# A chunked recurrence followed by a routed MoE: TensorE's steps reordered, scores of b in full quarters, old states by transposes

## The chip, the cores and the metric

The kernel runs on one core of one Trainium2 chip, in fp32. The metric is the device time of one execution in microseconds. The kernel before takes 818.32 us, the median of three runs (818.29, 818.32 and 825.19). The engines have short names in the profile: PE is TensorE, DVE is VectorE, ACT is ScalarE, POOL is GpSimd and SP is SyncE, which only issues transfers; PEld are TensorE's weight loads.

## The reference

There are two parts, one after the other. The first is a recurrence over S = 768 steps, for each of B = 4 batches and H = 8 heads, with a state of D x D = 40 x 40:

```
y[t]  = r[t] . state
Sa    = state . a[t]
state = state * w[t] - outer(Sa, b[t]) + outer(v[t], k[t])
```

Its output y, seen as B*S = 3072 tokens of H*D = 320 features, is the input of a mixture of experts. There are 8 experts, and a token's expert is fixed by a hash of its id, `token_ids * 2654435761 % 8`. Each expert computes `relu(x @ w1[e]) @ w2[e]` with an inner size of 1024.

## The kernel before

**Chunks.** The recurrence isn't walked step by step. The sequence is cut into 12 chunks of C = 64 tokens, and the batches into two pairs, which makes 24 tiles, u = 2n + g for chunk n and pair g; a tile has 16 heads (2 batches of 8). Within a chunk, cumulative products of the decays w (called p and q, q being taken from the other end) are multiplied onto a, b and k. Then the chunk's inner recurrence is a triangular system: the scores of b against a make a 64x64 unit triangular matrix per head, which is inverted and applied to a right side, built from the old state (r0) and from the chunk's own v and the scores of k (r1). The result c gives the new state (s) and, with the scores of r (rc_v for v, rc_c for c), the output y.

**The inverse.** A 64x64 triangle is treated as two diagonal blocks of BLK = 32 and one block below them. The diagonal blocks of four tiles (a group) are inverted together on VectorE, by 31 links of two instructions each (group_i, lines 506 and 509), with 128 partitions that hold 2 batches x 2 blocks x 32 rows. The transposes ut and ug of the result (lines 517, 518) feed the block below the diagonal, in two TensorE steps called x and u.

**The pipeline.** Tile u has an early part A (tile_a): its loads, the products with p and q, its transposes (at_t of a, z of b and k), and the scores a, from which ScalarE copies pk (the scores of b), GpSimd copies no (the part of pk below the diagonal blocks) and VectorE makes mk (the masked scores of k). Its late part runs LAG = 8 ticks later: tile_s (r and v, transposed in the step rv), tile_m (x and u) and tile_b (r0, r1, c, nc, rc, s, y, sd). nc are c's transposes, which go to the right operand of s; sd are the transposes of the decayed state sc, for the y of a later tick. So in ticks 8 to 23 every tick has part A of one tile and part B of another, and in the last eight ticks only part B.

**The order of the work.** Each piece is registered at a time, counted in ticks, by `at_tick`. The plan is sorted by that time and emitted in this order, and each engine executes its instructions in the order of emission. Within a tick the list STEPS (line 128) orders TensorE's steps; a step's copies by ScalarE, and what VectorE and GpSimd do for it, are emitted with it. The order of other work (loads, decays, the group's links) is set by numbers such as `t0 - 2`, `u - 2.3`. A TensorE step that has to wait holds all steps that follow.

**Decays.** p and q are made in rounds of two chunks (decays, lines 249 to 357), six in all. A round loads w, clamps it, makes prefix products on pb and suffix products on qb within segments (the chain; on VectorE for rounds 0 and 1, on GpSimd for later ones), takes the segments' products (own), combines them over TensorE (ends), and multiplies these into the segments (spread). Round 0 is turned on chip; later rounds are stored to p_rows and q_rows in memory by SP's queue, and each tile loads its part back (pl and ql). The code's instruction packets arrive by a queue of their own.

**PSUM.** The pool psa has two slots of two banks (for t_ps, z_ps, a_ps, c_ps and rc_ps), psb two slots of one bank (all other results of TensorE), psu one for the inverse. A slot is free for a new result when the copy that reads it is done.

**MoE.** From about 537 us the kernel loads the experts' weights, gathers each expert's tokens with indirect transfers and runs the two matmuls of each expert.

Of the kernel before, what the change touches and what calls it, by code (L numbers as in the profile page):

```python
# [8 lines left out]
F32 = mybir.dt.float32  # L9
I32 = mybir.dt.int32  # L10
AF = mybir.ActivationFunctionType
OP = mybir.AluOpType
# [6 lines left out]
def kernel(  # L19
# [108 lines left out]
    STEPS = ["c", "rc_v", "sd", "nc", "rc_c", "u", "a", "rv", "s", "x", "y", "z", "r0", "at_t", "r1"]  # L128
# [23 lines left out]
    for lo, hi, when in ((0, 4, -9.0), (4, LAG, -3.0), (LAG, NZ, 3.0)):  # L152
        @at_tick(when)
        def _(lo=lo, hi=hi):
            nc.gpsimd.memset(z_all[:, lo:hi].rearrange("p i b hp (two x) -> p (i b hp two) x", two=2)[:, :, D:C], 0.0)
# [4 lines left out]
    rv_r = ring("rv", 1, [P, 2, 3, HP, C])  # L160
    at_t_r = ring("at_t", LAG, [P, 2 * HP * C + BLK], lambda t: t[:, 2 * HP * C:], 4)
    r1_r = ring("r1", 2, [P, HP, R], gaps)
    r_r = ring("r", 2, [P, HP, P], gaps, 2)
# [4 lines left out]
    @at_tick(3.0)  # L168
    def _():
        nc.gpsimd.memset(x_all[:].rearrange("p i b hp (two x) -> p (i b hp two) x", two=2)[:, :, D:C], 0.0)  # L170
# [78 lines left out]
    def decays(ri, t_load, t0, t_own, t1):  # L249
# [3 lines left out]
        chain = nc.gpsimd if ri > 1 else nc.vector  # L253
# [10 lines left out]
        def clamp():  # L264
            chain.tensor_scalar(x["qb"][:, 0:HC * D], x["pb"][:], LO, HI, op0=OP.max, op1=OP.min)
            (nc.vector if fast else nc.gpsimd).memset(segs(x["pb"])[:, :, 0, :], 1.0)
# [39 lines left out]
        def turned(i, src):  # L306
# [4 lines left out]
            if i == 0:  # L311
                nc.scalar.copy(hi[half(0)], lo[half(1)])
                nc.scalar.copy(lo[half(1)], lo[half(0)])
            else:
# [6 lines left out]
        def finish():  # L321
            eng = nc.vector if fast else nc.gpsimd
            if fast:
                spread(eng, x["qb"][:], x["ends"][:, 1:])
                turned(0, x["qb"][:, D:])
                recip()
                spread(eng, x["pb"][:], x["own"][:])
                turned(1, x["pb"][:])
                return
            recip()  # L330
            for i, (t, by, src) in enumerate((("pb", x["own"][:], x["pb"][:]), ("qb", x["ends"][:, 1:], x["qb"][:, D:]))):
                spread(eng, x[t], by)
                for y in range(2 * RN):
                    nc.sync.dma_start(pq_dram[ri][i][y * HC:(y + 1) * HC].rearrange("t bh e -> bh t e"),
                                      src[y * BH:(y + 1) * BH].rearrange("p (t e) -> p t e", e=D))

        first_half = [clamp] + [lambda i=i: prefix(i) for i in range(1, SL)]
        second = [lambda i=i: suffix(i) for i in range(SL - 2, -1, -1)]
        if ri > 1:
            first_half += second  # L340
            second = []
        for i, f in enumerate(first_half):
            at_tick(t0 + (t_own - t0) * i / len(first_half), order=8)(f)
        at_tick(t_own, order=8)(own)
        for i, f in enumerate(second):
            at_tick(t_own + (t1 - t_own) * (i + 0.5) / (len(second) + 1), order=8)(f)
        at_tick(t1 - 0.05, order=8)(ends)
        at_tick(t1, order=8)(finish)

        @at_tick(t1 + 0.6, order=8)  # L350
# [12 lines left out]
    def tile_a(u):  # L363
# [8 lines left out]
        if early:  # L372
            t_in, t_pq, t_mul = -8.9 + 0.01 * u, None, -6.0 + 0.01 * u
            t_turn, t_a = u - 1, u + 0.9 if u < 3 else u + 0.4
        elif second:
            base = 4 + 0.7 * (u - 4)
            t_in, t_pq, t_mul, t_turn, t_a = u - 2.3, 3.4 + 0.01 * u, base - 0.5, base - 1, base + 0.4
        else:
            t_in, t_pq, t_mul, t_turn, t_a = u - 2.3, u - 2.7, u - 1.7, u - 1, u + STEPS.index("a") / len(STEPS)

        @at_tick(t_in)
        def _():
            x["z"] = z_r(u)
            x["at"] = r_r(1) if u == 3 else at_r(u)
# [22 lines left out]
        @at_tick(t_mul)  # L407
        def _():
            eng = nc.vector if early else nc.gpsimd
            if early:  # L410
                p, q = (rounds[0][i][rn] for i in "pq")
                x["p"] = p[:, (2 * g + rn) * DM:(2 * g + rn + 1) * DM]
# [3 lines left out]
            times(eng, x["at"][:], x["p"])  # L416

        @at_tick(t_turn, "at_t")
        def _():
            t = at_t_r(u)  # L420
            x["at_f"] = t
            x["at_t"] = t[:, 0:2 * HP * C].rearrange("p (b hp t) -> p b hp t", b=2, hp=HP)
# [3 lines left out]
            nc.scalar.copy(t[0:R, 0:2 * HP * C].rearrange("p (b c) -> p b c", b=2), p[0:R, :, 0:HP * C])  # L426

        @at_tick(t_turn, "z")
        def _():
            if early and u % 2:  # L430
                x["z_t"] = rv_r(0)[:, :, 0:2]
            else:
                x["z_t"] = work.tile([P, 2, 2, HP, C], F32, tag="z_t", name="z_t", bufs=1)
            p = psum("z_ps")
            for i in range(2):
                for be in range(2):
                    for hp in range(HP):
                        c0 = (be * HP + hp) * C
                        nc.tensor.transpose(p[0:R, i, c0:c0 + C], x["z"][half(i), be, hp, 0:R], ident[half(i), half(i)])  # L439
            nc.scalar.copy(x["z_t"][0:R].rearrange("p i b hp t -> p i (b hp t)"), p[0:R])  # L440

        @at_tick(t_a)
        def _():
            gi, ti = divmod(u, GRP)
            p = psum("a_ps")
            for hp, par, be in quarters():
                z = x["z_t"][half(par), be, be, hp, :]
                c0 = (be * HP + hp) * C
                for i in range(2):
                    r0 = be * C + i * BLK  # L450
                    mm(p[r0:r0 + BLK, par, hp * C:(hp + 1) * C], z[:, i * BLK:(i + 1) * BLK],
                       x["at_f"][half(par), c0 + i * BLK:c0 + i * BLK + C])
            for hp, par, be in quarters():
# [624 lines left out]
```

## Time and profile before

The profiled execution took 824.48 us, with a span of 822.7 us and a mean granted TensorE clock of 0.888.

| | us | share of the span |
|---|---|---|
| span | 822.7 | |
| PE busy | 653.1 | 79% |
| DVE busy | 324.1 | 39% |
| POOL busy | 282.4 | 34% |
| ACT busy | 259.1 | 31% |
| start, to the first y at 142.8 | 142.8 | 17% |
| 15 ticks with both parts, 142.8 to 437.2 | 294.4 | 36% |
| 8 ticks with part B alone, to 534.8 | 97.6 | 12% |
| MoE, to the end | 287.9 | 35% |

The rows of the stages were read from TensorE's timeline, by the start of each tile's y. Busy time is time in which an engine executes; the share of an engine over the whole span is a mean over these four stages. The granted clock is the share of its full speed at which TensorE was allowed to run. Its value in a short stretch is close to 0.5 or to 1.0. A line of a timeline gives the start, the duration, the engine, the source line, the operation, its output and inputs with their partitions x elements, the count of instructions, and in brackets the idle time before it and what ended that. Durations of neighbouring TensorE steps overlap a little, so that a step's cost is better taken from its start to the start of the next.

### The profile page before, as it was taken

To read this page: it belongs to the slowest core of one execution; us is meant where nothing else is said; L and a number is where in the kernel's file an instruction comes from. 1 tells how busy PE (TensorE), PEld (TensorE's weight loads), DVE (VectorE), ACT (ScalarE), POOL (GpSimd) and SP (SyncE) were. 2 spreads that over 40 slices of the span, in tenths; PEclk is the share of its full clock that TensorE was granted. 3 is DMA by queue.
4 is the path that set the end of the run, shared out by engine and by line. 5 is a ranking of instruction groups with operands and counts; after the bars stand their busy time and mean duration, and the time that the engine had idled before them with its cause. 6 is when DMAs were issued, how large, how long until landed. Compare 5 with 4: busy or idle time off the path is not lost.

```text
span 822.7 us, 27069 instructions
## 1 busy us (share of the span) xinstructions
PE 653.1 (79%) x11982; PEld 498.9 (61%) x11982; DVE 324.1 (39%) x709; ACT 259.1 (31%) x518; POOL 282.4 (34%) x372
## 2 busy tenths in 40 slices
PE   0534366979798898788888989929999999999993
PEld 0423355868687877677776878815555655655652
DVE  6674644663664356346525742211441101111110
ACT  0622233445444454455534445501011011111110
POOL 3057785264437464334212212240302202210101
PEclk9999997787878679899858879968989999999997
DMA  9455776634664477444212223188841343220000
GB/s 159 100 90 126 129 138 105 150 82 84 121 149 86 74 115 142 94 85 89 39 33 41 42 55 65 39 290 265 283 136 39 112 148 102 95 88 16 24 3 27
DMA packets 201896, 83.47 MB, mean 101 GB/s; under 512 B 177518, under 2 KB 192367, under 8 KB 201776
## 3 DMA queue, kind: packets, MB, share of 16 engines
q1 hardware_dynamic: 189008, 64.32, 36.3%
q0 software_dynamic: 6336, 16.08, 6.6%
q10 hardware_dynamic: 6432, 1.31, 1.0%
q8 instruction: 95, 1.56, 0.8%
q14 instruction: 25, 0.20, 0.1%
HBM read 66.56 MB, written 15.44 MB: 100 GB/s over the span
## 4 chain that ended last, share of the span: by engine, by line
PE 65%; DVE 9%; issue 9%; SPq 4%; POOL 4%; ACT 4%; DMA 3%; POOLq 0%; ACTq 0%; DVEq 0%
PE dn_ps L913 11%; PE up_ps L893 9%; PE r_ps L220 6%; PE y_ps L220 5%; PE s_ps L220 5%; PE rc_ps L220 4%; PE a_ps L220 4%; PE u_ps L220 3%; PE t_ps L475 3%; PE up_ps L889 3%; PE z_ps L439 3%; PE c_ps L220 3%; PE sd_ps L220 2%; PE nc_ps L635 2%; POOL xg L872 1%
## 5 line engine op out<-in xcount | busy, mean ns | idle before, releaser
L913 PE MATMUL dn_ps<-w,ht 128*128 128x320 f32 x384 | 104.9, 433 | 0.0
L893 PE MATMUL up_ps<-xt,w 128*128 128x416 f32 x256 | 96.0, 529 | 0.0
L913 PEld LDWEIGHTS dn_ps<-w,ht 128*128 128x128 f32 x384 | 72.8, 190 | 32.1 <-issue 1.9
L903 POOL DMA_INDIRECT out_dram<-o,idx_all x26 | 25.8, 992 | 189.6 <-ACT o L902 184.8
L684 POOL DMA_DIRECT2D x_rows<-xs x48 | 26.8, 562 | 157.2 <-DVE xs L681 105.0
L893 PEld LDWEIGHTS up_ps<-xt,w 128*128 128x128 f32 x256 | 48.5, 195 | 47.6 <-issue 47.6
L509 DVE TENSOR_TENSOR ub<-ub,outer 128x31 f32<-128x31 f32 (+15 forms) x186 | 65.0, 349 | 6.4
L439 PE MATMUL z_ps<-ident,z_all 64*128 64x64 f32 x384 | 34.8, 289 | 40.8 <-POOL z_all L405 31.0
L646 DVE TENSOR_TENSOR mr<-rc_ps,after 128x1024 f32<-128x1024 f32 x24 | 29.4, 1225 | 92.4 <-PE rc_ps L220 92.4
L506 DVE TENSOR_TENSOR outer<-ub,nb 128x31 f32<-128x31 f32 (+15 forms) x186 | 62.8, 338 | 4.2 <-ACT ub L491 0.3
L896 DVE TENSOR_SCALAR ht<-up_ps 128x416 f32<-128x416 f32 x32 | 18.9, 591 | 96.1 <-PE up_ps L893 91.7
L439 PEld LDWEIGHTS z_ps<-ident,z_all 64*128 64x128 f32 x384 | 29.8, 189 | 44.4 <-POOL z_all L405 33.3
L220 PE MATMUL a_ps<-at_t,z_t 64*32 64x64 f32 (+1 forms) x2112 | 40.1, 251 | 15.8 <-issue 9.4
L878 DVE COPY xt<-xg_ps 128x384 f32<-128x384 f32 x24 | 12.1, 551 | 101.7 <-PE xg_ps L877 94.2
L220 PEld LDWEIGHTS a_ps<-at_t,z_t 64*32 64x32 f32 (+1 forms) x2112 | 32.9, 132 | 21.9 <-issue 12.2
L440 ACT COPY z_t<-z_ps 128x1024 f32<-128x1024 f32 x22 | 22.3, 1012 | 70.7 <-PE z_ps L439 70.7
L405 POOL TENSOR_TENSOR z_all<-z_all,ql 128x320 f32<-128x320 f32 x40 | 34.1, 864 | 28.1 <-DMA z_all<-in_k_dram 22.2
L902 ACT COPY o<-dn_ps 128x320 f32<-128x320 f32 x24 | 10.2, 426 | 101.6 <-PE dn_ps L913 101.6
L872 POOL DMA_INDIRECT xg<-x_rows,src_all x26 | 27.3, 1050 | 29.8 <-PE xg_ps L877 15.7
L898 ACT ACTIVATE ht<-up_ps 128x416 f32<-128x416 f32 x32 | 15.9, 515 | 65.3 <-PE up_ps L893 65.3
L889 PE MATMUL up_ps<-xt,w 64*128 64x416 f32 x128 | 30.6, 580 | 7.1 <-DVE xt L878 3.2
L220 PEld LDWEIGHTS s_ps<-x_all,z_all 128*64 128x64 f32 x704 | 27.7, 159 | 13.6 <-issue 13.6
(190 smaller groups left out, 1228.8 us busy)
## 6 DMA issues: line engine op xcount, KB each, us to landing
w<-in_moe_w_dram SPq DMA_DIRECT2D x8, 1280.0 KB
w<-in_moe_w_dram SPq DMA_DIRECT2D x8, 1024.0 KB
ql<-q_rows SPq DMA_DIRECT2D x40, 160.0 KB
r<-in_r_dram SPq DMA_DIRECT2D x48, 80.0 KB
x_all<-in_v_dram SPq DMA_DIRECT2D x48, 80.0 KB
py<-p_rows POOLq DMA_DIRECT2D x48, 80.0 KB
x_rows<-xs POOLq DMA_DIRECT2D x48, 80.0 KB
wt<-in_w_dram SPq DMA_DIRECT2D x6, 640.0 KB
```

What stands on the lines that cost most here:

```text
L220: nc.tensor.matmul(out_, lhsT=lhsT, rhs=rhs, start=start, stop=stop, skip_group_check=True)
L405: eng.tensor_tensor(t, t, by.rearrange("p (h e) -> p h e", e=D), op=OP.mult)
L439: nc.tensor.transpose(p[0:R, i, c0:c0 + C], x["z"][half(i), be, hp, 0:R], ident[half(i), half(i)])
L506: nc.vector.tensor_tensor(tv, ub[:, 0:j + 1, j:j + 1].to_broadcast([P, j + 1, m]), nb[:, j, j + 1:].unsqueeze(1).to_broadcast([P, j + 1, m ...
L509: nc.vector.tensor_tensor(o, o, tv, op=OP.add)
L646: nc.vector.tensor_tensor(t[:].rearrange("p two h t -> p (two h) t"), p[:].rearrange("p two (h t) -> p (two h) t", t=C), after[:].unsqueez ...
L684: nc.gpsimd.dma_start(x_rows[r0:r0 + C, :], xs[half(be)])
L872: nc.gpsimd.indirect_dma_start(out=xg[:, 0:DM], out_offset=None, in_=x_rows[:], in_offset=bass.IndirectOffsetOnAxis(ap=idx, axis=0))
L889: nc.tensor.matmul(banks[-1][:], lhsT=w1[rows, w:w + P], rhs=xt[rows, 2, 0:n], start=True, stop=False)
L893: nc.tensor.matmul(p[:], lhsT=w1[:, c * F + f * P:c * F + (f + 1) * P], rhs=xt[:, c, 0:n], start=False, stop=(c == 1))
L903: st = nc.gpsimd.indirect_dma_start(out=out[:], out_offset=bass.IndirectOffsetOnAxis(ap=idx, axis=0), in_=o[:], in_offset=None, bounds_che ...
L913: nc.tensor.matmul(p[:], lhsT=ht[:, f, j * P:(j + 1) * P], rhs=w2[:, f, :], start=(f == 0), stop=(f == FP - 1))
```

## The change

**The order of the steps.** STEPS goes from `c, rc_v, sd, nc, rc_c, u, a, rv, s, x, y, z, r0, at_t, r1` to `c, z, rcc, nc, rcv, s, a, y, x, sd, r0, at_t, u, r1, rv`. The step x runs one tick before its tile's part B instead of two, and u late in the same tick. z of a tile is in the same tick as its a, and at_t in the tick before. rcc precedes rcv, and the mask product mr follows the latter.

**Scores of b.** In the profile a matmul of fp32 is two instructions and a transpose one. The step a had 32 matmuls for the scores of b, each making 32 of a quarter's 64 rows, and 16 of 64x64 for those of k (96 instructions); now both kinds are 16 full 64x64 matmuls (64 instructions). So the lower diagonal blocks lie in other columns than before, and ScalarE brings them to their place: it copies pk's 32 columns and then, for each batch, the lower rows again from shifted columns. The part no, which GpSimd copied from pk, is now copied by ScalarE from PSUM.

**Old states.** sd was 16 small matmuls (32 instructions) with the identity as the right operand, in a slot of psb; it is now 8 transposes, in a slot of psa.

**r, v and c.** The tile rv is split: the transposes of r go to rt, those of v into a tile cv that c is also copied to. ScalarE makes two copies of half the size where it had one. The transposes of c (nc) read cv.

**Decays and the start.** The parts of a round get times of their own (t_clamp, t_chain, t_own, t_ends, t_spread, t_store). The clamp of rounds 2 to 5 moves from GpSimd to VectorE. Round 2's own, ends, spread and store come after the elimination of group 0, which itself is planned over ticks 3.43 to 6.4. Stores of later rounds come about 0.8 of a tick later. The first tiles' loads, transposes and products, and two fills with zero on GpSimd, are planned in another order.

```diff
-    STEPS = ["c", "rc_v", "sd", "nc", "rc_c", "u", "a", "rv", "s", "x", "y", "z", "r0", "at_t", "r1"]
+    STEPS = ["c", "z", "rcc", "nc", "rcv", "s", "a", "y", "x", "sd", "r0", "at_t", "u", "r1", "rv"]
...
-    def decays(ri, t_load, t0, t_own, t1):
+    def decays(ri, t_load, t_clamp, t_chain, t_own, t_ends, t_spread, t_store):
...
-            chain.tensor_scalar(x["qb"][:, 0:HC * D], x["pb"][:], LO, HI, op0=OP.max, op1=OP.min)
+            nc.vector.tensor_scalar(x["qb"][:, 0:HC * D], x["pb"][:], LO, HI, op0=OP.max, op1=OP.min)
...
-            t_in, t_pq, t_mul, t_turn, t_a = u - 2.3, 3.4 + 0.01 * u, base - 0.5, base - 1, base + 0.4
+            t_in, t_pq, t_mul = (0.55, 0.97, 0.2, 1.05)[u - 4], 3.1 + 0.05 * (u - 4), base - 0.5
+            t_mulz = t_mul
+            t_z, t_at, t_a = base - 0.3, base - 0.15, base + 0.4
         else:
-            t_in, t_pq, t_mul, t_turn, t_a = u - 2.3, u - 2.7, u - 1.7, u - 1, u + STEPS.index("a") / len(STEPS)
+            t_in, t_pq, t_mul = u - 2.3, max(u - 2.4, 6.9 + 0.02 * (u - 8)), max(u - 1.7, 7.0)
+            t_mulz = t_mul
+            t_z, t_at, t_a = (u - i + STEPS.index(n) / len(STEPS) for i, n in ((0, "z"), (1, "at_t"), (0, "a")))
...
-            for hp, par, be in quarters():
-                z = x["z_t"][half(par), be, be, hp, :]
-                c0 = (be * HP + hp) * C
-                for i in range(2):
-                    r0 = be * C + i * BLK
-                    mm(p[r0:r0 + BLK, par, hp * C:(hp + 1) * C], z[:, i * BLK:(i + 1) * BLK],
-                       x["at_f"][half(par), c0 + i * BLK:c0 + i * BLK + C])
-            for hp, par, be in quarters():
-                mm(p[half(1 - be), par, (HP + hp) * C:(HP + hp + 1) * C], x["z_t"][half(par), 1 - be, be, hp, :],
-                   x["at_t"][half(par), be, hp, :])
+            for kind in range(2):
+                for hp, par, be in quarters():
+                    i = be ^ kind
+                    c0 = (kind * HP + hp) * C
+                    mm(p[half(i), par, c0:c0 + C], x["z_t"][half(par), be, hp, i, :], x["at_t"][half(par), be, hp, :])
...
-            nc.scalar.copy(pk.rearrange("p two hp t -> p two (hp t)"), p[:, :, 0:HP * C])
...
-            nc.gpsimd.tensor_copy(no[:], pk[:, :, :, BLK:C])
+            nc.scalar.copy(pk, pb[..., 0:BLK])
+            for be in range(2):
+                low = slice(be * C + BLK, (be + 1) * C)
+                nc.scalar.copy(pk[low], pb[low, :, :, BLK:])
...
+            nc.scalar.copy(no[:], pb[..., BLK:])
...
-        @at_tick(t0 - 2, "x")
+        @at_tick(t0 - 1, "x")
...
-            nc.scalar.copy(t[0:R, :, odd:odd + 2].rearrange("p i j hp t -> p i (j hp t)"), p[0:R])
+            nc.scalar.copy(t[:].rearrange("p b hp t -> p b (hp t)"), p[:, :, 0:HP * C])
+            nc.scalar.copy(cv[:, :, 2:4].rearrange("p hp b t -> p b hp t"),
+                           p[:, :, HP * C:].rearrange("p b (hp t) -> p b hp t", hp=HP))
...
-                p = bank([P, 2 * HP * D], "sd_ps")
+                p = psum("sd_ps")
...
-                        for par in range(2):
-                            rows = half(par)
-                            mm(p[half40(par), (be * HP + hp) * D:(be * HP + hp + 1) * D], sc[rows, be, hp, :],
-                               ident[rows, half40(par)])
+                        nc.tensor.transpose(p[0:D, be, hp * R:(hp + 1) * R], sc[:, be, hp, :], ident[:])
...
-    decays(0, -9.0, -8.0, -7.5, -7.0)
-    decays(1, -8.5, 0.1, 1.9, 3.35)
-    decays(2, 0.0, 3.36, 4.85, 5.2)
+    decays(0, -9.0, -8.0, (-7.9, -7.6), -7.7, -7.4, -7.2, None)
+    decays(1, -8.5, 0.1, (0.15, 1.85), 1.88, 2.2, 2.65, 2.7)
+    decays(2, -5.5, 0.45, (0.5, 2.5), 6.41, 6.43, 6.5, 6.6)
     for ri in range(3, NR):
-        decays(ri, ri * RN * NG - 7.0, ri * RN * NG - 6.3, ri * RN * NG - 4.2, ri * RN * NG - 4.0)
+        t = ri * RN * NG
+        decays(ri, t - 5.8, t - 5.3, (t - 5.2, t - 3.9), t - 3.75, t - 3.6, t - 3.55, t - 3.2)
...
-        group_i(gi, t0 + 0.05, t0 + 0.1, t0 + (3.0 if gi == 0 else 3.15))
+        if gi == 0:
+            group_i(gi, 3.43, 3.47, 6.4)
+        else:
+            group_i(gi, t0 + 0.05, t0 + 0.1, t0 + 3.1)
```

## The prediction

> **What bounds the kernel now.** I read the busy shares of the span first (PE 79%, DVE 39%, POOL 34%, ACT 31%), then the stages, which differ. Columns of the stretches: window, busy us of PE, PEld, DVE, ACT and POOL, granted clock, DMA share.
> ```profile
> core 0: us, PE busy (x) PEld busy (x) DVE busy (x) ACT busy (x) POOL busy (x), PEclk, DMA share, GB/s
> 0.00:142.80 142.80, 62.57 (x1494) 52.60 (x1494) 81.17 (x182) 44.40 (x86) 78.82 (x109) 0.96 0.65 121
> 142.80:437.20 294.40, 252.38 (x6948) 221.69 (x6948) 151.73 (x338) 136.27 (x258) 128.96 (x171) 0.80 0.50 95
> 437.20:534.80 97.60, 86.10 (x2532) 75.91 (x2532) 41.37 (x94) 45.70 (x91) 20.51 (x38) 0.90 0.27 50
> ```
> To 142.8 (the first y) the kernel fills its pipeline; then come 15 steady ticks of 19.63 us, then 8 drain ticks of 12.2. The steady part is TensorE's, at 86% busy, but at a granted clock of 0.80. TensorE's timeline of one tick at full clock:
> ```profile
> 382.02 1.01 PE L439 MATMUL z_ps<-ident,z_all 64*128 64x64 f32 x16
> 382.97 0.77 PE L220 MATMUL r_ps<-st,at_t 128*64 128x80 f32 x16
> ...
> 385.73 0.69 PE L220 MATMUL c_ps<-um,r 64*64 64x64 f32 x32 [0.53 <-issue]
> 386.25 1.03 PE L220 MATMUL rc_ps<-rv 64*64 64x64 f32 x32
> 387.07 0.80 PE L220 MATMUL sd_ps<-ident,sc 64*40 64x40 f32 x32
> 387.81 0.66 PE L635 MATMUL nc_ps<-ident,ct 128*128 128x128 f32 x4
> 388.39 0.69 PE L220 MATMUL rc_ps<-rv,ct 64*64 64x64 f32 x32
> ...
> 390.46 1.48 PE L220 MATMUL a_ps<-at_t,z_t 64*32 64x64 f32 x96
> 391.87 0.47 PE L475 MATMUL t_ps<-ident,r 64*128 64x64 f32 x8
> ```
> A step costs its start to the next start: c 0.52, sd 0.74, nc 0.58, a 1.41. From y (380.41) to the next y (395.44) it is 15.0 us, the best steady tick. Taking for every step the usual value of undisturbed ticks, the steps sum to 13.3 us, and with c's regular wait of 0.53 to 13.83. The same steps in half-clock stretches sum to 21.8. What stands between 13.83 and 19.63 are waits and the clock. TensorE's waits from 142 to 450 (us in total, times, longest):
> ```profile
> PE x_ps L220 <- DVE ut L517: 10.7, 4, 3.2
> PE a_ps L220 <- issue: 9.4, 8, 1.9
> PE c_ps L220 <- ACT r L611: 5.2, 10, 0.5
> ```
> and the clock, in stretches of 3.41 us (PE busy, instructions, granted clock):
> ```profile
> 277.10:280.52 3.42, 1.89 (x23) 0.99 0.05 9
> 280.52:283.93 3.41, 3.41 (x76) 0.50 0.00 0
> 283.93:287.34 3.41, 3.41 (x57) 0.50 0.02 5
> 297.58:301.00 3.42, 3.42 (x146) 1.00 0.61 105
> ```
> One stretch with a stall (1.89 busy) drops the clock, and it stays down though later ones are full. There are 13 such spells from 142.8 to 534.7, 136.5 us in all, 10.5 each. A half-clock microsecond does 13.3/21.8 = 0.61 of the work, so they lose 136.5 x 0.39 = 53 us: about 46 of the steady 294.4 (clock 0.80 means 40% at half), 3.06 per tick. The rest, 19.63 - 13.83 - 3.06 = 2.74, is stalls. Last, VectorE's timeline of the start:
> ```profile
> 74.09 0.33 DVE L275 TENSOR_TENSOR own<-pb,qb 128x160 f32<-128x160 f32 x1 [7.95 <-POOL pb L270]
> 89.51 0.32 DVE L292 TENSOR_TENSOR ends<-own,ex_ps 128x160 f32<-128x160 f32 x1 [10.36 <-ACT qb L291]
> 100.41 1.95 DVE L517 STREAM_TRANSPOSE ut<-ub 128x1024 f32<-128x1024 f32 x1
> 130.19 0.18 DVE L735 TENSOR_SCALAR eid<-tok 128x24 int32<-128x24 int32 x1 [6.38 <-DMA tok<-in_moe_token_ids_dram]
> ```
> Group 0's elimination takes 54.9 to 100.2 though its own work is 23.4 us: round 2's decays stand in the middle of it, waiting.
>
> **The start.** Group 0's chain now precedes round 2's own, so both waits (7.95 + 10.36) leave it. First inputs are loaded earlier, so pk is ready near 49.5; 23.4 us of work plus some interposed operations puts ut and ug at about 79 instead of 104. Next late is what was moved behind: round 2's own at 80, ends, two spreads on POOL (2.90 each) to 92, then 8 stores on SP's queue (some 0.65 each to issue, behind other loads) to 99.7, the loads of tile 8's p and q to 104.8, its three products on POOL (0.86 each) to 107.4. c(0) follows r1 and u near 111, z(8) 107.4; then mr must pass eid, which waits for tok, and round 3's own, which waits for POOL's chain (7.56 in a like place): mr 119.7, y(0) at 121 where it was 142.8. If those two waits hardly cost, 108; if tok stays at 130, y is at 130. I take 121: **-22**.
>
> **The steady tick.** From 13.83:
> - a: 96 instructions become 64 of c's kind. c has 32 for 0.52, so 1.04 instead of 1.41: -0.37.
> - sd: 32 instructions (0.74) become 8 transposes; nc's four take 0.58, so at most 1.16; with only 40 rows of output perhaps 0.6. I take 1.0: +0.28.
> - c's wait for r1's copy (0.53): rv now lies between, 0.71 of work: -0.53.
> - z comes second and needs the PSUM slot that rv leaves after its copies. These become two of 512 (0.587, by ACT's 512 copies) instead of one of 1012 ns; c covers 0.52 of about 1.3: +0.8. With c's output also needing a slot, up to 1.2; if the other slot is free, 0.
> - s: nc's two ACT copies (0.58 each and about 0.2 to pass) lie before it, covered by rcv 0.47 and s's first matmul 0.3-0.4: +0.3 (0 to 0.8). c and the rest: +0.1.
>
> Sum 14.4 without stalls. Stalls: ut is ready about a tick before x, and x is a tick later, so the 10.7 + 2.6 us (0.7 a tick) go; next late is x's user u, in the same tick behind y, sd, r0: x's copies (0.36 each) fit. Waits marked "issue" follow dense instruction runs: 0.5 to 1.9 each, just as a 16 KB instruction packet lands. Before, c to a is 520 instructions in 5.4 us, of 924 a tick; after, 812 a tick, 256 at most in some 2.9 us before sparse work. I keep 0.4 of 1.2. y's waits (xi, sc) stay inside +0.4.
>
> Other engines, per tick: ACT copies pk, its two shifted parts and no in 256 elements each (about 0.37, as um's and xi's copies) where it had one of 0.587, and rv costs 0.16 more: 9.06 + 0.9 + 0.16 + sd, some 10.4. DVE takes round clamps (2.06, once in four tiles, and it had them on POOL at 4.52) and waits less evenly: from 10.0 to about 11.5, in the group ticks near 90% of 14.4; this is the tightest. SP issues 11.1. POOL loses no (0.40) and the clamps. I put none of these on the path: TensorE's steps hide them, as they do now; without that cover ACT's added 1.3 a tick would cost 15 x 1.3 = 20 us, which is the third case below. The stores of a later round's p and q move 0.8 of a tick later, behind the next tiles' loads on SP's queue; they issue from 3.2 ticks before the tile that first reads them and its load goes out at 2.4, products at 1.7: 0.55 of a tick (8 us) from the last store to the first load, where 8 stores take 5 us to issue. I take nothing; if the queue is late, up to 5 us per round, 4 rounds: 20 us (the third case again). What waits behind DVE's mr, should mr wait for rc, is xs and the elimination's next link; neither is needed within two ticks.
>
> **The clock.** [...]
>
> Steady: 15 x (14.4 + 0.4 + 1.3) = 241.5, against 294.4: **-53**. Drain: the best full tick is 11.45 against 12.2 on average; rcc there waits for c's copy without z between, +0.55 x 8 = +4.4; clock (7.6 lost) halved -3.8, ut's last wait -2.6: **-2**. From 534.8 on the work is untouched: 0. Sum -77 against the span of 822.7 (execution 824.48, which is 6.2 above the median of the runs, 818.3): span 746. The median of the runs moves by the same: 818.3 - 77 = **742**.
>
> **Rivals.**
> - [...] 0.24.
> - Drops as before, or new waits of z's slot in their place: 15 x 18.0 = 270 (-24), start -22, drain 0: **772**; with half the start's gain lost it is alike. For it: DVE's busy group ticks. 0.20.
> - Slower: the sparse stretch keeps the clock at half. Place: x to rv of every tick and z, nc beside it. Price: about 23 us a full tick at half, 15 x 23 = 345 (+51), drain 8 x 18.5 = 148 (+50), start -22: **897**. It decides (time over 818) from 58% of the stretch at half, on the line from 742 (17%) to 897 (100%); before it was 35%. 0.04.
> - The main case, **742** (+-18), 0.50; no change 0.02.
>
> A change under 1% (8 us) can't be told from none here. Faster by over 1%: 0.94, within 0.02, slower 0.04. Range: the low end takes most of the vanishing case, 703; the high most of the third, 782.
>
> **What would show it.** y(0) near 121, ut near 79, no wait of own inside group 0's chain; y-to-y ticks of 14.5 to 15 at full clock; a step of 1.0; no ut wait; z waiting 0.5 to 1.2 for an ACT copy; clock in the steady part 0.88 to 0.95. Wrong if y(0) stays past 135, if z or s wait over 1.5 each tick, or if the clock stays at 0.8 or below.

## The result, and the profile after

The changed kernel takes 783.19 us (median, 777.86 to 785.14) where the kernel before takes 819.53 (818.29 to 825.19). The ratio is 0.953, with a 95% interval of 0.947 to 0.960. So it is 36 us faster, where 77 was forecast: the sign is right, the size is half, and the time lies just above the range of 703 to 782. Some runs of a kernel take over 1.5% longer than its fastest one (e2_own_apart: 781.98 beside 767.34); ratios and intervals leave these out, and so do the medians of the kernel before that stand with the experiments.

The stages of the profiled execution (span 780.4 us, execution 782.22); the columns are those of the stretches in the forecast: window, busy us of PE, PEld, DVE, ACT and POOL, granted clock, DMA share.

```profile
core 0: us, PE busy (x) PEld busy (x) DVE busy (x) ACT busy (x) POOL busy (x), PEclk, DMA share, GB/s
0.00:138.30 138.30, 52.92 (x1091) 45.99 (x1091) 81.61 (x176) 45.97 (x97) 60.22 (x88) 0.67 0.64 121
138.30:397.50 259.20, 234.20 (x6111) 200.38 (x6107) 161.94 (x348) 149.84 (x325) 118.25 (x155) 0.87 0.65 108
397.50:490.90 93.40, 83.29 (x2473) 72.54 (x2468) 43.24 (x93) 49.86 (x109) 21.45 (x39) 1.00 0.33 53
490.90:780.40 289.50, 253.47 (x1032) 149.48 (x1024) 50.28 (x97) 32.85 (x84) 53.86 (x54) 0.93 0.35 116
```

| stage | before | forecast | after | after - forecast |
|---|---|---|---|---|
| start, to the first y | 142.8 | 121 | 138.3 | +17.3 |
| 15 steady ticks | 294.4 | 241.5 | 259.2 | +17.7 |
| 8 drain ticks | 97.6 | 95.6 | 93.4 | -2.2 |
| rest | 287.9 | 287.9 | 289.5 | +1.6 |

By the starts of y, which are 438.24 for the end of the steady ticks and 534.2 for the last y, the stages of before are 295.4, 96.0 and 288.5 us; the table has them as they were read ahead of the forecast, and nothing below hangs on this 1 us.

So 34 us are missing, half of them in the start and half in the steady ticks. TensorE's timeline shows the steps of a steady tick at full clock:

```profile
369.66 1.05 PE L701 MATMUL sd_ps<-ident,sc 128*40 128x128 f32 x8
...
374.88 0.69 PE L220 MATMUL c_ps<-um,r 64*64 64x64 f32 x32
376.11 1.01 PE L452 MATMUL z_ps<-ident,z_all 64*128 64x64 f32 x16 [0.54 <-ACT cv L593]
377.06 0.69 PE L220 MATMUL rc_ps<-rt,cv 64*64 64x64 f32 x32
377.68 0.66 PE L654 MATMUL nc_ps<-ident,cv 128*128 128x128 f32 x4
...
381.59 1.16 PE L220 MATMUL a_ps<-at_t,z_t 64*64 64x64 f32 x64
382.69 0.78 PE L220 MATMUL y_ps<-sd,rt 128*64 128x80 f32 x16
```

From start to start, a takes 1.10 (forecast 1.04), sd usually 0.98 (1.0), and c with z's wait 1.23. Taken over all undisturbed ticks the steps sum to 14.05, less than the 14.4 of the forecast; the best whole tick is 14.09. At half clock the same steps sum to 23.3. What the tick loses lies in TensorE's waits of the steady part (total, times, longest):

```profile
PE z_ps L452 <- ACT cv L593: 5.9, 11, 0.5
PE x_ps L220 <- DVE ends L292: 3.1, 2, 1.7
PE ex_ps L220 <- DVE own L277: 2.4, 1, 2.4
PE y_ps L220 <- DVE mr L645: 2.4, 1, 2.4
PE r_ps L220 <- issue: 2.1, 2, 1.5
PE y_ps L220 <- issue: 2.0, 1, 2.0
PE sums_ps L751 <- DVE ends L292: 1.7, 1, 1.7
```

ut is gone from the list, and VectorE stands there with three other works, 9.6 us together. All waits of the stretch are 24.5 us: these 9.6, 6.9 marked issue, and 8.0 for ScalarE, of which z's are 5.9. The waits for own and mr come from VectorE's full queue: in the 12.4 us before the wait for mr ends, VectorE is busy for 11.85, and in the 12.0 before that for own ends for 11.16. The waits for ends are of another kind. ex_ps lies in one of psb's two slots until VectorE has read it for ends, and x and sums need a slot; VectorE itself waits there for ScalarE's copy:

```profile
285.56 0.32 DVE L292 TENSOR_TENSOR ends<-own,ex_ps 128x160 f32<-128x160 f32 x1 [0.63 <-ACT qb L291]
285.93 0.69 PE L220 MATMUL x_ps<-ut,no 32*32 32x32 f32 x32 [1.68 <-DVE ends L292]
```

In the 10 us before, VectorE is busy for only 4.17. So here no engine is overloaded: ex_ps is made at 278, but ScalarE's two copies of it stand in its queue behind those of a (pk and no) until 285.2, and ends waits for them. The wait for mr, and the clock in stretches of 3.4 us around it:

```profile
224.28 0.77 PE L220 MATMUL y_ps<-sd,rt 128*64 128x80 f32 x16
227.44 1.13 PE L220 MATMUL y_ps<-z_all,mr 128*64 128x40 f32 x32 [2.39 <-DVE mr L645]
```

```profile
222.00:225.45 3.45, 3.05 (x113) 1.00 0.87 165
225.45:228.87 3.42, 1.43 (x54) 1.00 0.77 137
228.87:232.28 3.41, 2.73 (x36) 0.50 0.69 121
235.69:239.11 3.42, 3.42 (x68) 0.50 0.93 106
245.93:249.35 3.42, 3.42 (x138) 1.00 1.01 229
```

The stretch with the wait is 1.43 busy, the next one runs at half clock, and the half clock lasts 17 us although TensorE is fully busy in most of it. In the whole steady part 64.9 us are at half clock, in seven spells. Four of the seven begin in or right after a wait for ends, own, mr and ends again: 13.7 + 6.8 + 17.1 + 3.4 = 41.0 us. The other three follow waits marked issue (1.46, 2.04 and 0.63 us).

The start as VectorE's timeline shows it, then two rows of TensorE's:

```profile
58.48 1.98 DVE L507 STREAM_TRANSPOSE nb<-pk 128x1024 f32<-128x1024 f32 x1
84.03 1.96 DVE L527 STREAM_TRANSPOSE ut<-ub 128x1024 f32<-128x1024 f32 x1
87.60 0.31 DVE L275 TENSOR_TENSOR own<-pb,qb 128x160 f32<-128x160 f32 x1
129.39 0.24 DVE L743 TENSOR_SCALAR eid<-tok 128x24 int32<-128x24 int32 x1 [30.42 <-DMA tok<-in_moe_token_ids_dram]
```

```profile
117.11 0.70 PE L485 MATMUL t_ps<-ident,at 64*128 64x64 f32 x8 [21.45 <-POOL at L414]
132.88 0.27 PE L220 MATMUL ex_ps<-own,ident 128*32 128x40 f32 x1 [5.38 <-DVE own L277]
```

Group 0's elimination now runs without a break, 58.5 to 87.6 with both transposes, as forecast. But the work behind it makes TensorE wait 21.45 us for tile 8's product with p, and then 5.38 for round 3's own. This second wait is there because VectorE, with own behind in its queue, stands 30.42 us in front of the token ids.

### The profile page after: what moved, and what is told of

It is laid out like the page before. It is cut to its first block, busy times and chain, and to the rows that moved or that the text cites. A ratio compares the mean times of both kernels' runs of the same rounds, so it can differ in the third digit from the quotient of the medians.

```text
span 780.4 us, 24437 instructions
## 1 busy us (share of the span) xinstructions
PE 623.9 (80%) x10686; PEld 468.4 (60%) x10686; DVE 337.1 (43%) x713; ACT 278.5 (36%) x614; POOL 253.8 (33%) x336
## 4 chain that ended last, share of the span: by engine, by line
PE 62%; issue 8%; DVE 6%; ACT 6%; DMA 3%; POOL 2%; SPq 2%; POOLq 0%; ACTq 0%; DVEq 0%
PE dn_ps L921 12%; PE up_ps L901 10%; PE r_ps L220 6%; PE s_ps L220 6%; PE y_ps L220 4%; PE rc_ps L220 4%; PE u_ps L220 3%; PE t_ps L485 3%; PE up_ps L897 3%; PE a_ps L220 3%; PE sd_ps L701 2%; PE z_ps L452 2%; PE nc_ps L654 2%; ACT rt L592 2%; DMA xg<-x_rows,src_all 1%
## 5 line engine op out<-in xcount | busy, mean ns | idle before, releaser
L901 PE MATMUL up_ps<-xt,w 128*128 128x416 f32 x256 | 97.7, 536 | 0.0
L921 PEld LDWEIGHTS dn_ps<-w,ht 128*128 128x128 f32 x384 | 72.8, 190 | 32.1 <-issue 1.9
L452 PE MATMUL z_ps<-ident,z_all 64*128 64x64 f32 x384 | 32.0, 277 | 29.9 <-POOL z_all L414 14.1
L452 PEld LDWEIGHTS z_ps<-ident,z_all 64*128 64x128 f32 x384 | 27.9, 180 | 33.4 <-POOL z_all L414 14.6
L910 ACT COPY o<-dn_ps 128x320 f32<-128x320 f32 x24 | 10.2, 426 | 101.6 <-PE dn_ps L921 101.6
L220 PE MATMUL rc_ps<-rt,cv 64*64 64x64 f32 x1536 | 38.1, 245 | 9.4 <-ACT cv L628 8.9
L220 PEld LDWEIGHTS rc_ps<-rt,cv 64*64 64x64 f32 x1536 | 31.1, 153 | 15.9 <-ACT cv L628 10.0
L674 ACT COPY st<-sc 40x320 f32<-40x320 f32 x44 | 20.1, 457 | 57.0 <-DVE sc L671 56.7
L880 POOL DMA_INDIRECT xg<-x_rows,src_all x26 | 27.2, 1044 | 30.5 <-PE xg_ps L885 15.8
L220 PE MATMUL a_ps<-at_t,z_t 64*64 64x64 f32 x1408 | 32.2, 251 | 3.6 <-ACT at_t L438 2.6
```

Source lines behind the costliest of these rows:

```text
L220: nc.tensor.matmul(out_, lhsT=lhsT, rhs=rhs, start=start, stop=stop, skip_group_check=True)
L452: nc.tensor.transpose(p[:, i, c0:c0 + C], x["z"][half(i), be, hp, :], ident[half(i), half(i)])
L880: nc.gpsimd.indirect_dma_start(out=xg[:, 0:DM], out_offset=None, in_=x_rows[:], in_offset=bass.IndirectOffsetOnAxis(ap=idx, axis=0))
L901: nc.tensor.matmul(p[:], lhsT=w1[:, c * F + f * P:c * F + (f + 1) * P], rhs=xt[:, c, 0:n], start=False, stop=(c == 1))
L921: nc.tensor.matmul(p[:], lhsT=ht[:, f, j * P:(j + 1) * P], rhs=w2[:, f, :], start=(f == 0), stop=(f == FP - 1))
```

## The experiments

The kernel before ran beside each set of four or three; its medians were 823.3, 821.7, 817.8 and 827.8 on the four occasions. The changed kernel, too, has the ratio 0.953 in its first comparison and 0.942 beside the fourth set. So a difference of some 10 us between sets says nothing, and runs of one set are compared where that matters. The first set is the runs to e4, the second to e8, the third to e12; the changed kernel itself ran only in the fourth.

**Token ids earlier.**

```diff
+    @at_tick(1.2)
+    def _():
+        nc.sync.dma_start(tok[:], ...)
     def routing():
-        nc.sync.dma_start(tok[:], ...)
```

> The changed kernel with one transfer moved: the token ids are loaded at tick 1.2 instead of tick 8 on SP's queue. In the changed kernel VectorE stands 30.4 us (98.9 to 129.4) in front of them, with group 1's elimination behind, and TensorE waits 5.4 us for own before the first y. Theory A (VectorE's late work holds TensorE back): the first y comes at 131 to 134 instead of 138.3, group 1's elimination ends before 125, the first steady ticks lose some of their waits, and the time falls by 6 to 14 us, to about 772. Theory B (the start is bound by round 2's store and load, the rest by the clock and the code): the 30 us are idle time of an engine that isn't needed; the first y stays within 2 us and the time is 780 to 784.

779.6 us (ratio 0.952, 0.941 to 0.962), first y at 135.9. Nearer to theory B, but the edit didn't take the wait away. VectorE's row:

```profile
125.51 0.36 DVE L749 TENSOR_TENSOR mine<-eid,iota_e 128x192 f32<-128x192 int32 x1 [25.69 <-POOL iota_e L742]
```

eid was done at 99.8, and the instruction behind it waited for a row of indices that GpSimd makes in its order, after products that wait for round 2's q. The wait had a second cause behind the first.

**Own and ends of later rounds apart.**

```diff
+        at_tick(t_cross or t_own, order=8)(cross)   # the matmuls that read own
...
-        decays(ri, t - 5.8, t - 5.3, (t - 5.2, t - 3.9), t - 3.75, t - 3.6, t - 3.55, t - 3.2)
+        decays(ri, t - 6.1, t - 5.6, (t - 5.5, t - 4.4), t - 4.2, t - 3.92, t - 3.55, t - 3.2, t - 3.98)
```

> The changed kernel with rounds 3 to 5 of the decays arranged otherwise: POOL's chain 0.5 tick earlier, own at t - 4.2 instead of t - 3.75, the matmuls that read it at t - 3.98 (after c, where no result of psb is due) and ends at t - 3.92 instead of t - 3.6. In the changed kernel TensorE waits in the steady part 2.4 us for own and 3.1 us in step x for ends, each followed by a half-clock spell. Theory A: these waits go (5 us), and the spells after them (13.7 + 6.8 + 3.4 us at half clock, worth 0.4 of that, 9 us): 768 to 776. Theory B: other waits trigger the clock in their place, and the time is 779 to 784.

770.2 us (0.934, 0.924 to 0.944), in the range of theory A, and 9 us less than e1_tok_early in the same set. The steady ticks take 245.6 us instead of 259.2:

```profile
140.20:385.80 245.60, 220.28 (x6111) 188.77 (x6107) 155.51 (x346) 150.07 (x323) 115.47 (x154) 0.94 0.67 115
```

The waits for ends and mr are gone, one of own (2.4) is left, and the half-clock time is 27.3 us instead of 64.9. But all of TensorE's waits in these ticks are 25.0 us where they were 24.5: others stand in their place, u and en for xs (3.3) and more of those marked issue (10.7 for 6.9). So in this profile the gain lies in the clock and not in the waits. The half-clock time isn't steady enough to prove that it came from the edit: e1_tok_early and e4_old_rounds, which keep the changed kernel's order of steps and have 9.3 and 14.5 us of waits for VectorE, have 42.5 and 44.4 us of it.

**Dense order.**

```diff
-    STEPS = ["c", "z", "rcc", "nc", "rcv", "s", "a", "y", "x", "sd", "r0", "at_t", "u", "r1", "rv"]
+    STEPS = ["c", "x", "rcc", "sd", "nc", "rcv", "u", "a", "s", "y", "z", "r0", "at_t", "r1", "rv"]
...
-            ... for i, n in ((0, "z"), (1, "at_t"), (0, "a"))
+            ... for i, n in ((1, "z"), (1, "at_t"), (0, "a"))
```

> The changed kernel with the steps of a tick grouped as before in kind: c, x, rcc, sd, nc, rcv, u, a, then s, y, z, r0, at_t, r1, rv (z in the tick before its a). All else as changed; no step waits for ut. If alternating dense and sparse groups is what brought the steady part down, stalls marked issue come back in u and a (before: 9.4 us in a) with drops of the clock, half-clock time in the 15 steady ticks goes from 65 us to 100 or more, and the time is 795 to 810. If the order is not the cause and the gain is from the removed waits and instructions: 778 to 788, with z's wait of 0.54 per tick gone as its only effect (-8).

764.6 us (0.930, 0.920 to 0.939): faster than the changed kernel, against both expectations, and 15 us less than e1_tok_early in the same set. The half-clock time is 30.7 us, so dense neighbours don't pull the clock down here, and alternating groups don't keep it up. The best tick is 13.64 instead of 14.09, as z no longer waits for its slot. The drain takes 85.2 us instead of 93.4: in the changed kernel and in this one, a drain tick has the wait

```profile
430.88 0.69 PE L220 MATMUL rc_ps<-rt,cv 64*64 64x64 f32 x32 [1.08 <-ACT cv L628]
```

```profile
425.65 0.69 PE L220 MATMUL rc_ps<-rt,cv 64*64 64x64 f32 x32 [0.46 <-ACT cv L628]
```

(first the changed kernel, then the dense order, where x lies between c and rcc). Their y steps are 12.05 and 11.23 apart.

**Old times of the later rounds.**

```diff
-        decays(ri, t - 5.8, t - 5.3, (t - 5.2, t - 3.9), t - 3.75, t - 3.6, t - 3.55, t - 3.2)
+        decays(ri, t - 7.0, t - 6.3, (t - 6.2, t - 4.3), t - 4.2, t - 4.05, t - 4.0, t - 3.95)
```

> The changed kernel with the times of rounds 3 to 5 put back to about those of before: load t - 7.0, clamp t - 6.3, own t - 4.2, ends t - 4.05, store t - 3.95; the chain stays on POOL and the clamp on VectorE. If the new times of these rounds are what makes TensorE wait for own and ends: 770 to 778. If they only moved a wait that is anywhere the same: 780 to 786. If the later stores were needed: slower, 788.

780.7 us: the same. The wait only moved: TensorE now waits 9.2 us in y for sc, and 3.9 for own. So it isn't enough that these works are earlier; it seems to matter in which step of TensorE's they fall.

**All three.** The edits of the three runs e1, e2 and e3 together.

> Three edits at once on the changed kernel: token ids loaded early, own and ends of later rounds moved apart, and the dense order of steps (c, x, rcc, sd, nc, rcv, u, a, s, y, z, r0, at_t, r1, rv). Alone they gave medians of 779.6, 770.2 and 764.6 where the changed kernel has 783.2. If their gains add (each removes its own wait): 783 - 4 - 13 - 18 = 748. If they remove the same thing, VectorE's lateness in the ticks of a group, the time stays near the best one, 760 to 765.

776.2 us (0.933, 0.918 to 0.948), with 54.6 us at half clock, where 748 was expected if the gains add. They don't. In the dense order r0 waits 6.9 us for sc, and own and ends, now near x, aren't what waits; why it is no faster than the dense order alone stays open.

**The kernel before, with x a tick later.**

```diff
-    STEPS = ["c", "rc_v", "sd", "nc", "rc_c", "u", "a", "rv", "s", "x", "y", "z", "r0", "at_t", "r1"]
+    STEPS = ["c", "x", "rc_v", "sd", "nc", "rc_c", "u", "a", "rv", "s", "y", "z", "r0", "at_t", "r1"]
...
-        @at_tick(t0 - 2, "x")
+        @at_tick(t0 - 1, "x")
```

> The kernel before with the step x one tick later and right after c; nothing else. If the waits of x for ut (10.7 us from 142 to 450, 13.3 in all) and the clock spells behind them are a large part of the gain: all of x's waits go, and with about a third of the 116 us of half-clock time in the steady part: 818 - 13 - 15 = 790. If the next wait takes their place (u for x's copies, or the stalls of code): 805 to 815.

797.6 us (0.963, 0.943 to 0.983), between the two expectations. This one step is worth 24 us beside the kernel before of its set (821.7), where the whole change has 36; the interval allows 14 to 47. It takes x's waits for ut away without any other part of the change: in the steady ticks the waits for VectorE go from 16.3 us to 1.4 and the half-clock time from 116 to 75, while those marked issue rise from 18.0 to 27.2.

**Old scores of b.**

```diff
-            for kind in range(2):
-                for hp, par, be in quarters(): ...
+            for hp, par, be in quarters(): ...   # 32 matmuls of 32 rows, then 16 of 64, as before
...
-            nc.scalar.copy(no[:], pb[..., BLK:])
+            nc.gpsimd.tensor_copy(no[:], pk[:, :, :, BLK:C])
```

> The changed kernel with the step a as before: 96 instructions, of which 64 make 32 rows each, one copy of pk by ScalarE, no by GpSimd. By the start-to-start times of a at full clock, 1.41 against 1.09, a tick is 0.32 us longer, 20 ticks 6 us. Theory C (instructions are what counts: 128 more a tick through the queue that brings code, 16% more packets, more stalls before dense steps and more drops of the clock): 795 to 805. Theory D (only the columns count): 786 to 790. With ScalarE's shorter copies, 0.9 per tile, of worth in place: 780.

778.7 us (0.944, 0.930 to 0.958): no slower. From start to start a takes 1.42 us instead of 1.09, and all waits of the steady ticks are 30.5 us instead of 24.5 (the best tick, with a wait of 0.66 for r's copy in it, is 15.14). But the half-clock time is 27.3 us instead of 64.9, and the two cancel. Neither theory C nor D said this. Whether this came with the 32 instructions more in each a, or with the slower ticks, in which the waits for VectorE fall from 9.6 us to 1.6, one profile doesn't decide.

**Old states by matmuls**, in a slot of psb as before, and then in a slot of psa:

```diff
-                p = psum("sd_ps")
+                p = bank([P, 2 * HP * D], "sd_ps")      # e8; psum("sd_ps")[:, 0, 0:2 * HP * D] in e9
-                        nc.tensor.transpose(p[0:D, be, hp * R:(hp + 1) * R], sc[:, be, hp, :], ident[:])
+                        for par in range(2):
+                            mm(..., sc[rows, be, hp, :], ident[rows, half40(par)])
```

> The changed kernel with the old states by 16 small matmuls in a slot of psb instead of 8 transposes in a slot of psa. Step sd at full clock took 0.74 before and takes 0.98 with transposes, so 0.24 less per tick: 778. [...] If the matmuls' 24 instructions more in each tick, or the slot of psb, matter: 785 to 792.

> The changed kernel with the old states by the 16 matmuls of before, but in a slot of psa, where the changed kernel has its transposes; the same matmuls in a slot of psb gave 808.8, with 11.7 us of waits in sd for the copies of xi and 102 us of half-clock time. If it is the slot (x, sd and r0 are neighbours and share psb's two slots, and the wait between sparse steps drops the clock): the waits go, and the time is 776 to 786, as with transposes. If matmuls with 40 columns of output are worse for the clock or the order than transposes: 795 to 810.

In psb 808.8 us (0.983, 0.971 to 0.995), in psa 786.0 (0.964, 0.956 to 0.972). The two ran in different sets, but the difference is over what sets differ by, and e8_old_sd is also 30 us behind e7_old_a of its own set. So it is the slot. With psb, the chief wait and the steady stage are

```profile
PE sd_ps L220 <- ACT xi L550: 11.7, 11, 1.3
```

```profile
138.80:418.10 279.30, 246.22 (x6449) 214.40 (x6441) 162.15 (x348) 150.52 (x326) 118.14 (x155) 0.82 0.59 101
```

sd follows x, both in psb's two slots, so it waits for xi's copies, 1 us in each tick, and in the middle of the sparse steps. Beside e9_old_sd_in_psa, which differs in the slot alone, its steady ticks take 12.9 us more (279.3 and 266.4). The waits of sd are some 14 us, but all waits only 32.1 against 29.0; the half-clock time is 102 us against 75.1, which by the step sums is worth 11 us. So most of these 12.9 us lie in the clock. The 8 transposes themselves are as good as the 16 matmuls, as far as these runs can tell: 64.9 and 68.3 us at half clock with them, 75.1 without.

**The start arranged otherwise.**

```diff
-    decays(2, -5.5, 0.45, (0.5, 2.5), 6.41, 6.43, 6.5, 6.6)
+    decays(2, -5.5, 0.45, (0.5, 2.5), 3.05, 3.1, 3.12, 3.18)
...
-                at_tick(t_store + 0.25 * i, order=8)(lambda i=i: store(i))
+                at_tick(t_store + (0.01 if ri == 2 else 0.25) * i, order=8)(lambda i=i: store(i))
...
-            t_in, t_pq, t_mul = u - 2.3, max(u - 2.4, 6.9 + 0.02 * (u - 8)), max(u - 1.7, 7.0)
+            t_in, t_pq, t_mul = u - 2.3, max(u - 2.4, 6.5 + 0.02 * (u - 8)), max(u - 1.7, 6.6)
...
+    # tok, iota_e and token at tick 1.2
```

> The changed kernel with its start arranged otherwise: round 2's own, ends, spread and stores before group 0's elimination (ticks 3.05 to 3.2) where they come after it, tile 8's p and q loaded at tick 6.5, and the token ids and both index rows of the routing made at tick 1.2. With the token ids alone moved, VectorE still stood 25.7 us, then for GpSimd's iota_e, which is queued behind products that wait for round 2's q. Theory A' (the start is set by the trip own, spread, store, load, product of round 2, which begins only when group 0's chain ends, at 88): z and at of tile 8 are ready before 95, the first y comes at 108 to 118, and the time falls by 20 to 27 us: 755 to 765. If another wait takes its place (SP's queue, r and v, group 1): first y at 125 to 135, 772 to 780.

758.7 us (0.932, 0.921 to 0.942), 24 us less than the changed kernel, and the first y at 115.2. VectorE's and TensorE's rows:

```profile
55.58 2.77 DVE L275 TENSOR_TENSOR own<-pb,qb 128x160 f32<-128x160 f32 x1
89.13 1.95 DVE L527 STREAM_TRANSPOSE ut<-ub 128x1024 f32<-128x1024 f32 x1
101.72 0.36 DVE L749 TENSOR_TENSOR mine<-eid,iota_e 128x192 f32<-128x192 int32 x1
```

```profile
100.33 0.70 PE L485 MATMUL t_ps<-ident,at 64*128 64x64 f32 x8 [3.43 <-POOL at L414]
```

Round 2's own costs group 0 five us (ut at 89.1 instead of 84.0), and its p and q are back in time: TensorE's wait of 21.45 shrinks to 3.43, and the 30 us in front of the routing are gone. Theory A' is confirmed, with both causes named in it taken away together; the trip without the token ids and index rows wasn't run.

**The new start with the dense order.**

> The start of the run e10_start and the dense order of e3_dense_order (764.6) together. The two act in different stages, so their gains should add: 764.6 - 22 = 743 by theory A', 755 to 762 if another wait takes the start's place.

741.6 us (0.907, 0.894 to 0.920), on the same chip as the run before this one: the order is worth 17 us there, as it was 15 beside e1_tok_early in the first set. This kernel is faster than both the kernel before and the changed one.

**Only z and x moved.**

```diff
+    STEPS = ["c", "x", "rcc", "nc", "rcv", "s", "a", "y", "z", "sd", "r0", "at_t", "u", "r1", "rv"]
...
+            ... for i, n in ((1, "z"), (1, "at_t"), (0, "a"))
```

> The changed kernel with two steps moved: z behind y (in the tick before its a), and x behind c; so c, x, rcc, nc, rcv, s, a, y, z, sd, r0, at_t, u, r1, rv. u stays late among transposes, a among s and y. The dense order gave 764.6. If what the dense order took away are waits (z for its slot, 0.54 per tick; in the drain rcc for c's copy, 1.08 per tick, which x and sd covered): about 0.9 per tick less, with their spells, 764 to 770. If it is the grouping itself that matters to the clock or the code: 776 to 786.

778.0 us. z's wait for its slot is gone, but others are there (rcc for c's copy 5.7 us, mr 3.2, sd for no's copy 2.4); the best tick is 14.20 and the drain 91.8. So moving z alone doesn't give the dense order's gain; which of its neighbours does was not separated further.

**New start and own apart, in the changed kernel's order**, beside the changed kernel and the dense order with the new start, on one chip:

> The changed kernel, in its own order of steps, with both edits: the start of e10_start and own, ends of rounds 3 to 5 apart as in e2_own_apart. If the prediction's shortfall is these two (the start's trip behind group 0, and TensorE waiting for VectorE's own and ends), they add: 758.7 - 13 = 746, with 15 steady ticks in 242 to 248 us. If own and ends were not the cause in the steady part and e2_own_apart was luck with the clock: 756 to 762.

> The changed kernel as it is, for comparison on the same chip: 778 to 785. The half-clock time in its 15 steady ticks was 65 us in one execution, and 43 to 48 in executions of kernels with the same steady part (e4_old_rounds, e1_tok_early, e10_start); a second profile of the same kernel tells how much of the difference between kernels is chance: 40 to 65 expected.

> The dense order with the new start, on the same chip as the other two: 738 to 745. If alternating groups were of use, e13_start_own, which has them and has no wait for own, would be faster than this; if the dense order is better by its shorter ticks (13.64 against 14.09 us at full clock) and its shorter drain (85 against 94 us), it stays 5 to 15 us ahead.

751.2 (0.906, 0.899 to 0.912), 781.6 (0.942, 0.936 to 0.947) and 746.9 us (0.903, 0.896 to 0.910). The two edits together give 30 us. The first y is at 116.3, and the steady ticks are

```profile
116.30:366.30 250.00, 228.10 (x6112) 195.34 (x6105) 156.74 (x350) 149.97 (x322) 118.05 (x155) 0.90 0.66 113
```

so own and ends are worth 8.5 us in these ticks here (258.5 in e10_start, of another set) and 7.4 in the first set (253.0 in e1_tok_early). But here the half-clock time is 47.8 us in both, and the waits fall, from 30.4 to 21.3; in the first set it was the other way round. The gain came twice; by which path is open. The last run is 4 us ahead of e13_start_own, within the intervals: with own and ends apart, the two orders can't be told apart. The second profile of the changed kernel has its half-clock spells at the same places as the first: at 143.8, 201.8, 229.1 and 287.1, after the same waits for VectorE, of 13.7, 6.8, 17.1 and 3.4 us, again 41.0. So within this kernel these spells are not chance. What they cost depends on more than the wait: e1_tok_early and e10_start have almost the same waits for VectorE (9.3 and 9.5 us) and 42.5 and 47.8 us at half clock in all. Those after waits marked issue vary (10.2 and 17.1 where it was 10.2, 3.4 and 10.2).

## Why the prediction was wrong in its size

- **The tick without stalls** (14.4) was right, and a little long: 14.05. a, sd, c's wait and z's slot came out within 0.1 to 0.3 of their terms, and s's term of 0.3 was not there. 15 x (14.05 - 14.4) = -5 us.
- **The start failed** (-22; measured -4.5). The step is "pk is ready near 49.5". Group 0's chain is free of waits, as said, and as long as said (29.3 us with both transposes). But it began at 58.5, and every term that was added up behind it came 8 to 10 us late: own 87.6 for 80, spread 100.8 for 92, products 117 for 107. The last two a before it began at 51.3 and 53.1, at half clock (1.98 us each), with ScalarE's copies behind and with two waits for round 1's decays ahead, 3.99 us for own and 2.84 for e; how the nine us divide among these was not separated. Round 2's trip (own, spread, store, load, product) was on the path and was moved behind the chain. I took its terms from the right rows, but set their first one too early. On top, y waits for own behind the token ids, until 132.9; this I had named as the upper bound (y at 130). With the trip before the chain and the token ids and index rows early (e10_start), y came at 115.2, earlier than the 121 of the forecast; the token ids alone brought 2.4 us (e1_tok_early).
- **Stalls failed** (0.4 a tick; measured 1.5). The step is "I put none of these on the path": VectorE at 11.5 of 14.4 us per tick was called the tightest and then priced at nothing. It is busy for 161.9 of 259.2 us in this stage, which hides that its queue is full in a group's ticks, so that own and mr come late (4.8 us of TensorE's waits); and ends, over ScalarE and VectorE, holds the slot that x and sums need (another 4.8). TensorE's step sum at full clock (15 x 14.05 = 210.8) and the half-clock loss (64.9 x (1 - 14.05/23.3) = 25.8) leave 259.2 - 210.8 - 25.8 = 22.6 us of waits where I had 6. The 6 were meant for waits marked issue, and these are 6.9: what was missing is 9.6 for VectorE, 2.1 for ScalarE beside z's, and 4 that the list of waits does not name. In the stage's 17.7 us the tick counts -5, the stalls +17 and the clock +6.
- **The clock** (1.3 a tick; measured 25.8/15 = 1.7) had about the right size, in part by luck: the 1.3 was an estimate of mine for the sparse stretch x to rv, and no run shows it. In the profile after, the drops follow waits, and 41 of 65 us follow the waits for own, mr and ends. With own and ends moved 27 us were left, and the dense order, which the forecast saw as the source of stalls, has 31; but profiles of four kernels with the same steady part (the changed one, e1_tok_early, e10_start, e14_changed_again) range from 42.5 to 68.3, so one profile measures this only roughly. Nor is a fully busy stretch enough to bring the clock back here: the one from 235.69, 3.42 of 3.42 us busy, stays at 0.50, and the one from 225.45, busy for 1.43 of 3.42, is followed by a drop. No harm by the transposes can be seen either: 64.9 and 68.3 us at half clock with them, 75.1 with matmuls in the same slot (e9_old_sd_in_psa).
- **Drain and rest** came within about 2 us, the drain with two terms that cancel: its wait of rcc was 1.08 and not 0.55, and its clock loss zero. In the second profile of the changed kernel (e14_changed_again) it had some 12 us at half clock and took 100.8 us, so the near hit is in part luck.
- **The rivals.** The third (new waits, the start's gain half lost, 772) was the nearest case, and its mechanism is what happened, though it named z's slot and ScalarE beside VectorE. The slower case did not come. That an order like that of before, with x moved, would be better than the new one was in none. The forecast gave the alternation credit in the code stalls (0.4 for 1.2), which came out (0.46), and named z's slot and the drain's rcc as its costs; but the dense order, with own and ends as they are, is 15 to 17 us faster. And the moved step x gives 24 us by itself (e6_before_x_late), so by the medians some 12 of the 36 are left for all other parts of the change. For full quarters and transposes, e7_old_a and e9_old_sd_in_psa show no gain.

## What to carry to other kernels

When a queue is written by hand, price each instruction that is moved by what stands around it on its engine at that moment, not by the engine's mean load: an engine busy 62% of a stage still made another wait, as its work came in bunches. Look also at what a short trip over several engines holds while it lasts, here a slot of PSUM. A trip through memory (store, load, product) belongs in front of long work that doesn't need its result, and a wait for another engine can cost more than itself: here 2.4 us for mr were followed by 17.1 at half clock, by the step sums a loss of 6.8. And before an order of steps is credited with a gain, run the rest of the change in the old order.

## What was not expected of the hardware

- The profile of before has its first clock record at 126.9 us and shows full speed until then, so that its start has 0.96. But the durations there are those of half clock: from 26.8 to 104.4 us a whole z took 1.60 to 1.95 us and a 2.24 to 2.27 (1.01 and 1.48 at full clock). In the changed kernel, at a recorded 0.50 from 60 to 120 us, z took 1.60 to 1.94 and a 1.98. By this, TensorE ran at half speed through most of the start in both kernels, and the 0.67 of the changed kernel's start is no loss beside it.
- A wait of some 1 us in most ticks between sparse steps (e8_old_sd) came with 27 us more of half clock than e9_old_sd_in_psa has, while all waits together grew by 3 us.
- The half-clock spells behind waits for VectorE came at the same times in two executions of the changed kernel, to 0.3 us.
